# Seventy-two weight columns instead of 128 in one product of a gated feed-forward kernel

## The chip, the cores and the metric

The kernel runs on one NeuronCore of a Trainium2 chip; the other seven are idle. The metric is the device time of one execution in microseconds (us). TensorE multiplies a stationary operand (the weights, which a LDWEIGHTS instruction puts into the array) with a moving operand (the data, which a MATMUL streams through it) and adds the result up in a PSUM bank. The profile calls the matmuls PE and the weight loads PEld; DVE is VectorE, ACT is ScalarE, POOL is GpSimd, SP issues the DMAs.

## The reference

A softmax over seven taps weights seven neighbouring positions of `x` (an attention with a window of 7, eight heads), and the result goes through a gated feed-forward layer with 1,536 hidden channels and 192 output channels, for 16,384 positions. Cut to what matters here, with `a` the output of the window:

```python
w = softmax(weight_gen, axis=-1)                    # 7 taps, 8 heads
a[t] = sum_k w[t, :, k] * x_pad[t + k]              # 16384 x 192
gate = 1.0 / (1.0 + np.exp(-(a @ w_gate)))          # 192 -> 1536
val  = a @ w_val
out  = (gate * val) @ w_out                         # 1536 -> 192
```

## The kernel before, in words

**Tiling.** Positions are cut into 32 blocks of 512, hidden channels into 12 groups of 128. One block with one group is a unit, 384 in all. Per unit, `main_jobs` multiplies the 192 channels of `a` with the gate's and the value's weights (two PSUM banks, `g` and `v`); ACT makes the sigmoid `sg`, DVE the product `h`; and `out_jobs` multiplies `h` with the output weights into two further banks, `ph` for output channels 0 to 127 and `pt` for channels 128 to 191, which add up over the 12 units of a block.

**Two parts of each number.** The operands of the matmuls are of type fp32r, and each number is split into a high and a low part of that type. `hh` and `hl` are those of `h`; a weight tile `W[f]` holds high columns and, from column `LO` on, low ones. For the first 128 output channels there are three products, named head: high weights with `hh`, low weights with `hh`, high weights with `hl`. For the last 64 channels high and low weights stand side by side and make one 128-column operand, `both_`: columns 0 to 63 are high, 64 to 127 low. Two products are then enough, named tail: `both_` with `hh`, and `both_` with `hl`. The upper half of `pt` (low weights) is added to the lower at the end (`evac`).

**Row halves.** Each matmul contracts only 64 rows. The array holds two at a time, one on rows 0 to 63 (`LOW`) and one on rows 64 to 127 (`UP`). The program always issues them alternately, so that they run in pairs; such a pair is called a slot. A unit has 18 main and 10 output matmuls, hence 14 slots. `period(s)` writes them: the main products of unit `s`, mixed with the output products of unit `s - 2`, first those of the upper half (`up`, beside gate products) and later those of the lower half (`low`, beside value products). Each half of the array thus gets one tail product with `hl` per unit.

**Turns.** Both halves write `ph` and `pt`. Where the writing half changes, `emit` puts a tiny memset on POOL (`seen`, line 839) that waits for the last matmul of one half, and the first of the other waits for it.

**Order.** A planner (`Plan.run`) fixes the order of all engines' instructions when the program is built, from estimated durations; `SLOT` is the estimate for a slot. `emit` (line 841 issues every one of these matmuls) writes the jobs of a step in the order of the lists that `out_jobs` and `main_jobs` return. `ending` writes the last two units' output products without main products beside them.

Of the kernel before, what the change touches and what calls it, by code (L numbers as in the profile page):

```python
# [217 lines left out]
def conv_gated_ffn(ctx: ExitStack, tc: tile.TileContext, xt, wg, wcat, outT):  # L218
# [12 lines left out]
    nc = tc.nc  # L231
# [7 lines left out]
    R = P // 2  # L239
# [546 lines left out]
    def keys(u):  # L786
        n, f = units[u]
        return dict(
            A=("A", n), As=("As", n), T=("T", n), g=("gv", u, 0), v=("gv", u, 1), sg=("sg", u),
            h=("h", u), hh=("hh", u), hl=("hl", u), ph=("ph", n), pt=("pt", n),  # L790
        )
# [12 lines left out]
    def out_jobs(u, r, head_first, last=False):  # L804
        k, (n, f) = keys(u), units[u]
        rows = (LOW, UP)[r]
        w = W[f][rows, :]
        hi, lo = w[:, CB : CB + P], w[:, LO + CB : LO + CB + P]
        both_ = w[:, CB + P : CB + 2 * P]
        head = [(k["ph"], hi, "hh"), (k["ph"], lo, "hh"), (k["ph"], hi, "hl")]  # L810
        tail = [(k["pt"], both_, "hh"), (k["pt"], both_, "hl")]
        begin = f == 0 and r == 1
        jobs = []
        for part in (head, tail) if head_first else (tail, head):
            for i, (dst, w, t) in enumerate(part):
                jobs.append(
                    (dst, w, k[t], rows, None, begin and i == 0,
                     last and i == len(part) - 1)
                )
        return jobs  # L820
# [7 lines left out]
    def emit(slots):  # L828
        def f(buf, e):
            for pair in slots:  # L830
                for job in pair:
                    if job is None:
                        continue
                    dst, w, t, rows, x, start, stop = job
                    m = buf[t][rows, :] if x is None else buf[t][rows, x, :]
                    r, prior = writer.get(dst, (rows.start, None))
                    turn = None
                    if r != rows.start:
                        turn = nc.gpsimd.memset(seen, 0.0)  # L839
                        tc.add_manual_dep(turn.ins, prior.ins.name, SYNC, reason="end of a turn")  # L840
                    ins = nc.tensor.matmul(buf[dst], w, m, start=start, stop=stop)  # L841
                    if turn is not None:
                        tc.add_manual_dep(ins.ins, turn.ins.name, SYNC, reason="next turn")
                    writer[dst] = (rows.start, ins)

        return f
# [10 lines left out]
    def period(s):  # L857
# [8 lines left out]
        if u < 0:  # L866
            jobs, gv = list(zip(G, V)), [k["g"], k["v"]]
            for i in range(3):
                b = c = pe(
                    jobs[3 * i : 3 * i + 3], conv_op[f]["done"] + ready[n, i],  # L870
                    alloc=[] if i else [("gv", g) for g in gv],
                    uses=[xs[i]] + (gv if i else []), due=due[s, 2],
                )
        else:
            last = fo == NF - 1
            up = out_jobs(u, 1, True)
            low = out_jobs(u, 0, True, last)
            hs = [ko["hh"], ko["hl"]]
            po = [ko["ph"], ko["pt"]]
            gv = [k["g"], k["v"]]  # L880
            pe(
                list(zip(G[:2], V[:2])), deps, alloc=[("gv", k["g"]), ("gv", k["v"])], uses=xs,
                due=due[s, 0],
            )
            pe(
                list(zip(G[2:7], up)), conv_op[fo]["done"] + u_op[u],
                alloc=[("ph", po[0]), ("pt", po[1])] if fo == 0 else [],
                uses=xs + hs + gv + ([] if fo == 0 else po), due=due[s, 1],
            )
            b = pe(list(zip(G[7:], V[2:4])), [], uses=xs + gv, due=due[s, 2])  # L890
            c = pe(list(zip(low, V[4:])), [], uses=xs + hs + po + gv, due=due[s, 3])
            if last:
                evac(no, [c])
# [24 lines left out]
    def ending():  # L918

        a, b = len(units) - 2, len(units) - 1  # L920
        la, ua = out_jobs(a, 0, True), out_jobs(a, 1, False)
        lb, ub = out_jobs(b, 0, True), out_jobs(b, 1, False, True)
        lb[4] = lb[4][:-1] + (True,)
        ub[1] = ub[1][:-1] + (False,)
        X = None
        ka, kb = keys(a), keys(b)
        po = [ka["ph"], ka["pt"]]
        cf = conv_op[units[b][1]]["done"] + conv_op[units[a][1]]["done"]
        pe(
            list(zip(la, [ua[0], ua[1], X, ua[2], ua[3]])), cf + u_op[a],  # L930
            uses=[ka["hh"], ka["hl"]] + po, due=due[len(units), 3],
        )
        c = pe(
            list(zip(lb + [X, X], [ub[0], ub[1], X, ua[4], ub[2], ub[3], ub[4]])), u_op[b],
            uses=[ka["hh"], ka["hl"], kb["hh"], kb["hl"]] + po, due=due[len(units) + 1, 3],
        )
        evac(units[b][0], [c])
# [108 lines left out]
```

## Time and profile before

| | |
|---|---|
| median of 3 runs | 1303.37 us (1303.14 to 1305.34) |
| the profiled execution: span | 1304.0 us |
| PE busy | 1269.9 us (97%), 10,860 matmuls |
| PEld busy | 1068.8 us (82%), 10,860 weight loads |
| DVE, ACT, POOL busy | 1040.3, 615.6, 131.2 us |
| chain that ended last | PE 78%, DVE 17%, rest 5% |
| mean granted clock of TensorE | 0.992 |

The busy times are sums over the whole span, and matmuls overlap one another, so that 97% does not tell by itself what limits PE. Timelines are read in order of start: the distance from one slot's start to the next is the pace. A clock of 1.00 is the upper of TensorE's two levels (2.4 GHz), 0.50 the lower (1.2 GHz).

### The profile page before, as it was taken

Reading aid. Unit: us, or ns where it says so; the run is one execution under the profiler, and the core shown is the slowest. Engines: PE = TensorE matmul, PEld = TensorE weight load, DVE = VectorE, ACT = ScalarE, POOL = GpSimd, SP = SyncE. Lnnn points to the kernel's source line nnn. Section 1 sums busy time; section 2 is a strip of 40 time slices with the busy share of each in tenths; the row PEclk is TensorE's granted clock in tenths of the full one; section 3 lists DMA queues with packets and bytes.
Section 4 is the critical chain, followed back from the end, with each engine's and each line's share of the span. In section 5 each row is a group of like instructions: output and inputs, shape, how many; then the busy total and the mean of one; then the engine's idle time right before and its main releaser. Section 6 shows DMA issues by size and latency. Waiting matters only on the chain.

```text
span 1304.0 us, 29730 instructions
## 1 busy us (share of the span) xinstructions
PE 1269.9 (97%) x10860; PEld 1068.8 (82%) x10860; DVE 1040.3 (80%) x1904; ACT 615.6 (47%) x1040; POOL 131.2 (10%) x1477
## 2 busy tenths in 40 slices
PE   4989999999999999999999999999999999999998
PEld 2768788888877888888888888888888888888886
DVE  8889979999998788777778877777887777786443
ACT  4855745455454444444444444444444444444443
POOL 0000011111100111111111111111111111111110
PEclk9999999999989999999999999999999999999999
DMA  4675189798864454344445434444543444211100
GB/s 123 168 192 117 40 170 170 167 188 164 193 146 116 115 134 120 89 118 114 115 117 134 115 96 114 117 114 119 134 116 91 118 116 111 57 38 38 37 13 14
DMA packets 56482, 148.94 MB, mean 114 GB/s; under 512 B 10640, under 2 KB 28176, under 8 KB 56336
## 3 DMA queue, kind: packets, MB, share of 16 engines
q1 hardware_dynamic: 56336, 147.04, 48.1%
q8 instruction: 86, 1.41, 0.5%
q14 instruction: 60, 0.49, 0.1%
HBM read 108.86 MB, written 16.14 MB: 96 GB/s over the span
## 4 chain that ended last, share of the span: by engine, by line
PE 78%; DVE 17%; issue 2%; ACT 2%; DMA 1%; POOL 0%; DVEq 0%; SPq 0%; POOLq 0%; ACTq 0%
PE bank L841 76%; DVE acc L638 3%; DVE h L899 3%; DVE hl L905 3%; DVE prod L624 3%; DMA x<-in_x 1%; PE bank L408 1%; DVE m L458 1%; DVE acc L624 0%; DVE prod L677 0%; DVE acc L697 0%; DVE m L484 0%; DVE w L465 0%; DVE osb L951 0%; DVE cr L394 0%
## 5 line engine op out<-in xcount | busy, mean ns | idle before, releaser
L841 PE MATMUL bank<-hh,W 64*128 64x512 f32 x2304 | 772.2, 389 | 2.9 <-ACT hh L902 2.1
L841 PE MATMUL bank<-As,W 64*128 64x512 f32 x2304 | 650.2, 389 | 1.3 <-ACT As L732 0.7
L841 PE MATMUL bank<-T,W 64*128 64x512 f32 x2304 | 647.9, 388 | 2.0 <-ACT T L775 1.8
L841 PE MATMUL bank<-hl,W 64*128 64x512 f32 x1536 | 596.1, 389 | 1.8 <-DVE hl L905 1.6
L902 ACT CAST hh<-h 128x512 fp32r<-128x512 f32 x384 | 238.4, 621 | 518.0 <-DVE h L899 516.6
L841 PE MATMUL bank<-A,W 64*128 64x512 f32 x2304 | 474.8, 389 | 2.8 <-DVE h L899 2.4
L841 PEld LDWEIGHTS bank<-hh,W 64*128 64x128 f32 x2304 | 425.0, 185 | 43.2 <-issue 3.6
L841 PEld LDWEIGHTS bank<-T,W 64*128 64x128 f32 x2304 | 425.4, 185 | 41.1 <-ACT T L775 2.5
L841 PEld LDWEIGHTS bank<-As,W 64*128 64x128 f32 x2304 | 424.2, 185 | 40.2 <-ACT As L735 1.3
L899 DVE TENSOR_TENSOR h<-bank,sg 128x512 f32<-128x512 f32 x384 | 263.8, 687 | 158.2 <-PE bank L841 151.9
L905 DVE TENSOR_TENSOR hl<-h,hh 128x512 fp32r<-128x512 f32 x384 | 264.1, 688 | 86.8 <-ACT hh L902 83.0
L841 PEld LDWEIGHTS bank<-A,W 64*128 64x128 f32 x2304 | 291.2, 185 | 43.4 <-DVE h L899 3.3
L841 PEld LDWEIGHTS bank<-hl,W 64*128 64x128 f32 x1536 | 283.9, 185 | 29.8 <-DVE hl L905 4.6
L896 ACT ACTIVATE sg<-bank 128x512 f32<-128x512 f32 x384 | 229.8, 599 | 111.7 <-PE bank L841 107.3
L839 POOL MEMSET seen<- 1x1 f32 x1471 | 130.5, 89 | 1166.0 <-PE bank L841 1165.8
L638 DVE TENSOR_TENSOR acc<-acc,prod 128x512 f32<-128x512 f32 (+1 forms) x372 | 204.1, 552 | 0.9
L624 DVE TENSOR_TENSOR prod<-x,wb 128x512 f32<-128x512 f32 x186 | 122.8, 685 | 0.0
L624 DVE TENSOR_TENSOR prod<-xt,wt 128x256 f32<-128x256 f32 x186 | 77.4, 418 | 0.0
L759 DVE TENSOR_TENSOR T<-acc,T 64x256 fp32r<-64x256 f32 x64 | 26.7, 417 | 1.4 <-ACT T L756 0.4
L408 PE MATMUL bank<-ce,eye 128*128 128x512 f32 (+1 forms) x48 | 19.7, 496 | 7.3 <-DVE prod L677 6.0
L948 ACT COPY ev<-bank 64x512 f32<-64x512 f32 x32 | 18.7, 584 | 16.9 <-PE bank L841 16.9
L756 ACT CAST T<-acc 64x256 fp32r<-64x256 f32 x64 | 25.8, 403 | 0.8
(54 smaller groups left out, 359.9 us busy)
## 6 DMA issues: line engine op xcount, KB each, us to landing
wb<-ws SPq DMA_DIRECT2D x62, 896.0 KB
wt<-ws SPq DMA_DIRECT2D x62, 448.0 KB
As<-A SPq DMA_DIRECT2D x56, 256.0 KB
x<-in_x SPq DMA_DIRECT2D x32, 259.0 KB
out<-osb SPq DMA_DIRECT2D x32, 256.0 KB
T<-T SPq DMA_DIRECT2D x56, 128.0 KB
raw<-in_w SPq DMA_DIRECT2D x12, 576.0 KB
xt<-in_x SPq DMA_DIRECT2D x64, 65.5 KB
```

The source lines that it names most:

```text
L408: nc.tensor.matmul(dst, eye[:, 0].bitcast(F32), buf[E].bitcast(F32)[:, a:z], start=True, stop=False)
L624: nc.vector.tensor_tensor(out=buf[prod(k)][:, :cols].rearrange("p (i t) -> p i t", t=M2), in0=buf[X][:, k : k + cols].rearrange("p (i t) - ...
L638: ENG[e].tensor_tensor(out=a, in0=a, in1=buf[prod(k)][:, :cols], op=ALU.add)
L756: nc.scalar.copy(buf[T][rows, 0, own], buf[ACT_][rows, :M2])
L759: ENG[e].tensor_tensor(out=buf[T][rows, 1, own], in0=buf[ACT_][rows, :M2], in1=buf[T][rows, 0, own].bitcast(F32), op=ALU.subtract,)
L839: turn = nc.gpsimd.memset(seen, 0.0)
L841: ins = nc.tensor.matmul(buf[dst], w, m, start=start, stop=stop)
L896: nc.scalar.activation(out=buf[k["sg"]], in_=buf[k["g"]], func=AF.Sigmoid)
L899: nc.vector.tensor_tensor(out=buf[k["h"]], in0=buf[k["v"]], in1=buf[k["sg"]], op=ALU.mult)
L902: nc.scalar.copy(buf[k["hh"]], buf[k["h"]])
L905: ENG[e].tensor_tensor(out=buf[k["hl"]], in0=buf[k["h"]], in1=buf[k["hh"]].bitcast(F32), op=ALU.subtract)
L948: nc.scalar.copy(buf[EV][LOW, :], buf[PT][UP, :])
```

## The change

The tail product with `hl` takes only the first 72 of the 128 columns of `both_`: the 64 high ones and 8 of the low ones. Its result goes to partitions 0 to 71 of `pt`. The low weights' product with the low part of `h` is thereby left out for 56 of 64 channels. For the lower half (`r == 0`) the two tail products change places, so that the full-width one stands last.

```diff
@@ out_jobs
-        tail = [(k["pt"], both_, "hh"), (k["pt"], both_, "hl")]
+        tail = [(k["pt"], both_, "hh"), (k["pt"], both_[:, : R + 8], "hl")]
+        if r == 0:
+            tail.reverse()
@@ emit
-                    ins = nc.tensor.matmul(buf[dst], w, m, start=start, stop=stop)
+                    ins = nc.tensor.matmul(
+                        buf[dst][: w.shape[-1]], w, m, start=start, stop=stop
+                    )
```

`R` is 64. Every other engine's instructions, and all waits, are the same in the same order; 1,152 of PE's rows differ, three per unit. On PE, in the second half of one unit's slots in the middle of the program, the rows before are these (a number after a name is that of a buffer, `W_6` belongs to main products and `W_4` to output products; each row gives the output's shape and the semaphores waited for):

```order
L841 MATMUL bank_113<-As1_87,W_6_120 128x512
L841 MATMUL bank_113<-hl1_98,W_4_118 128x512
L841 MATMUL bank_113<-T1_89,W_6_120 128x512
L841 MATMUL bank_113<-hh1_95,W_4_118 128x512 [waits Pool_49]
L841 MATMUL bank_113<-T1_89,W_6_120 128x512
L841 MATMUL bank_113<-hl1_98,W_4_118 128x512
L841 MATMUL bank_113<-T1_89,W_6_120 128x512
L841 MATMUL bank_113<-A1_85,W_7_121 128x512 [waits Activation_49]
```

And now, on PE at the same place:

```order
L843 MATMUL bank_113<-As1_87,W_6_120 128x512
L843 MATMUL bank_113<-hl1_98,W_4_118 128x512
L843 MATMUL bank_113<-T1_89,W_6_120 128x512
L843 MATMUL bank_113<-hl1_98,W_4_118 72x512 [waits Pool_49]
L843 MATMUL bank_113<-T1_89,W_6_120 128x512
L843 MATMUL bank_113<-hh1_95,W_4_118 128x512
L843 MATMUL bank_113<-T1_89,W_6_120 128x512
L843 MATMUL bank_113<-A1_85,W_7_121 128x512 [waits Activation_49]
```

The narrow product stands where the wide one with `hh` stood, with the same wait for POOL, and the one with `hh` comes a slot later; in the upper half's slots only the width of one row changes.

## Rows read from the trace of the kernel before

**Rows 1.** The page's first part: busy us, share of the span, instructions.

```profile
PE 1269.9 (97%) x10860; PEld 1068.8 (82%) x10860; DVE 1040.3 (80%) x1904; ACT 615.6 (47%) x1040; POOL 131.2 (10%) x1477
```

**Rows 2.** The chain that ended last, from 411 us on: start, length, what.

```profile
411.15 883.20 PE bank L841 x7776
1294.35 0.04 issue
```

**Rows 3.** Stretches of time: length, busy us (instructions) by engine, clock, DMA share, GB/s.

```profile
412.00:414.00 2.00, 2.00 (x12) 1.62 (x10) 0.77 (x2) 0.60 (x1) 0.09 (x1) 0.50 0.00 0
417.00:800.00 383.00, 383.00 (x3382) 327.83 (x3380) 298.25 (x542) 171.79 (x293) 40.79 (x463) 1.00 0.47 115
800.00:1294.00 494.00, 494.00 (x4362) 422.75 (x4360) 354.69 (x634) 219.19 (x372) 52.50 (x596) 1.00 0.34 84
```

**Rows 4.** Groups from 417 to 1294 us: busy, mean ns, idle before.

```profile
L841 PE MATMUL bank<-hl,W 64*128 64x512 f32 x1106 | 426.9, 386 | 0.0
...
L841 PEld LDWEIGHTS bank<-hl,W 64*128 64x128 f32 x1106 | 203.5, 184 | 18.0
```

**Rows 5.** Timeline of PE, upper clock: start us, length us, instruction.

```profile
801.18 0.39 PE L841 MATMUL bank<-As,W 64*128 64x512 f32 x1
801.19 0.39 PE L841 MATMUL bank<-hh,W 64*128 64x512 f32 x1
801.41 0.39 PE L841 MATMUL bank<-As,W 64*128 64x512 f32 x1
801.42 0.39 PE L841 MATMUL bank<-hl,W 64*128 64x512 f32 x1
801.64 0.39 PE L841 MATMUL bank<-T,W 64*128 64x512 f32 x1
801.65 0.39 PE L841 MATMUL bank<-hh,W 64*128 64x512 f32 x1
```

**Rows 6.** Timeline of PEld, the same place.

```profile
801.41 0.18 PEld L841 LDWEIGHTS bank<-T,W 64*128 64x128 f32 x1
801.42 0.18 PEld L841 LDWEIGHTS bank<-hh,W 64*128 64x128 f32 x1
```

**Rows 7.** Timeline of PE at the lower clock level.

```profile
412.39 0.62 PE L841 MATMUL bank<-A,W 64*128 64x512 f32 x1
...
413.67 0.62 PE L841 MATMUL bank<-As,W 64*128 64x512 f32 x1
```

**Rows 8.** Timeline of PEld: loads for 64-wide, then for line 841's matmuls.

```profile
40.32 0.19 PEld L409 LDWEIGHTS bank<-W,eye 128*128 128x128 f32 x1
40.43 0.19 PEld L410 LDWEIGHTS bank<-cr,eye 128*128 128x128 f32 x1
40.67 0.18 PEld L841 LDWEIGHTS bank<-A,W 64*128 64x128 f32 x1
40.67 0.18 PEld L841 LDWEIGHTS bank<-hh,W 64*128 64x128 f32 x1
40.77 0.19 PEld L841 LDWEIGHTS bank<-As,W 64*128 64x128 f32 x1
```

**Rows 9.** Timeline of PE, the same place and the slots behind it.

```profile
40.46 0.28 PE L410 MATMUL bank<-cr,eye 128*128 128x64 f32 x1
40.67 0.50 PE L841 MATMUL bank<-A,W 64*128 64x512 f32 x1
40.67 0.50 PE L841 MATMUL bank<-hh,W 64*128 64x512 f32 x1
41.01 0.40 PE L841 MATMUL bank<-As,W 64*128 64x512 f32 x1
41.01 0.40 PE L841 MATMUL bank<-hh,W 64*128 64x512 f32 x1
41.25 0.39 PE L841 MATMUL bank<-As,W 64*128 64x512 f32 x1
```

**Rows 10.** Timeline of PE in the ending: matmuls without a partner.

```profile
1298.15 0.62 PE L841 MATMUL bank<-hh,W 64*128 64x512 f32 x2
1298.62 0.39 PE L841 MATMUL bank<-hl,W 64*128 64x512 f32 x1
```

**Rows 11.** Timeline of POOL: the memset of a turn and its wait.

```profile
801.01 0.09 POOL L839 MEMSET seen<- 1x1 f32 x1 [0.37 <-PE bank L841]
```

## The prediction

> **What bounds the kernel now.** The first part of the page [rows 1] has PE busy for 97% of the span and DVE for 80%; this says only where to look. The chain of waits decides: from 411.15 us it is one piece of 883.20 us and 7,776 matmuls, all of line 841, and behind it only the ending is left [rows 2]. In the table of stretches PE is busy without a break from 417 to 1294 us at a granted clock of 1.00, while DVE is busy for 78% and 72% of it [rows 3], and the groups of that stretch show no idle time before any matmul [rows 4]. So for 68% of the span (883.20 of 1304.0) the time is a count of slots times the pace of a slot, and nothing else on the chip matters. Before 411 us PE and DVE take turns on the chain; the same slots run there, and I count what a slot gains or loses there as an upper bound only.
>
> The pace: 883.20 / 3,888 slots is 0.2272 us. The timeline shows it slot by slot: the two matmuls of a slot start 0.01 us apart, and the next pair starts 0.23 us later, whatever the operand is (801.18, 801.41, 801.64) [rows 5]. At the lower clock level three slots take 413.67 - 412.39 = 1.28 us, 0.427 each [rows 7], at a clock of 0.50 [rows 3]. Were all of it paced by TensorE's clock, the upper level would halve it to 0.2133. The measured pace is 0.0139 us longer. A slot is thus 0.213 us of streaming 512 columns and some 0.014 us of something that the lower clock hides, call it the change-over.
>
> Is it the weight load? A load takes 0.184 us by the record [rows 4], starts as the matmul ahead of it starts, and has ended some 0.04 us before the slot after it begins (801.41 + 0.18 against 801.64) [rows 5, 6]. Even that length is mostly latency: where the matmuls are only 64 wide, a load follows the one before after 0.11 us (40.32, 40.43) [rows 8], so that this is what a 128-column load costs where nothing covers it. The loads of the two halves run at the same time: after a stop two start at 40.67, the next at 40.77 [rows 8], and both halves' second matmuls start together at 41.01 [rows 9]. One half's matmuls without a partner keep no better pace: two from 1298.15 and the next at 1298.62 are two steps of 0.235 [rows 10]. A load therefore has about 0.12 us to spare in each slot, and the partner costs nothing.
>
> **The change part by part.**
>
> *Narrower loads.* 768 loads, one per unit in each half, have 72 columns in place of 128. If the cost goes with columns, 0.11 us becomes 0.062, and 768 x 0.048 = 37 us of load work goes. All of it lies under the matmul ahead, with 0.12 us to spare, so I put it at 0. The cover is missing only in the ending, where a load after a stop lies open: at most five times 0.05 us, 0.25 us by this estimate, and I take 0.1.
>
> The Trainium skill ("TensorE: Matmul & The Clock Gate", section on LDWEIGHTS) gives the load's time as its columns at 1.2 GHz: 107 ns for 128, 60 for 72. The step of 0.11 us in rows 8 agrees with the first; no row here has the second. By the page the saving would be 47 ns a load, hidden all the same.
>
> *Narrower matmuls.* The same 512 columns of data stream through, so 0.213 us of the slot stays. Whether the change-over depends on the width of the weights the trace can't tell, since every load in it has 128 columns. From above: it does not, gain 0. From below: it vanishes for the narrow ones, 384 x 0.0139 = 5.3 us (each half has one per unit, and both halves must gain, or the faster waits for its partner; where only the slots from 411 us count, 278 units, 3.9 us). In between, in proportion to columns: 56/128 x 0.0139 = 6.1 ns, times 384, 2.3 us. I take 0: the change-over disappears at the lower clock [rows 7], so it isn't steps of the array, one per weight column, and the records fit a fixed time beside the stream better.
>
> *The swap in the lower half.* The first tail product of the half waits for the POOL memset of a turn. The memset for it starts at 801.01 and takes 0.09 us [rows 11]; the load that stands there starts at 801.42 [rows 6], 0.32 us later. The narrow product now takes this place with the same wait, and its operand `hl` was already used by the slot before. The turn to the other half ends with the same slot as before. Cost 0. Nothing is moved on DVE, ACT, POOL or SP.
>
> *Sum.* Span of the profiled execution 1304.0 - 0.1 = 1303.9; that execution lies 0.6 us above the median of 1303.37, so the median stays at 1303.3.
>
> **The rivals.**
>
> *The change-over follows the width.* 1303.4 - 2.3 = 1301.1 in proportion, 1298.1 if it goes away wholly. For it: nothing in the trace has another width. Against it: rows 7.
>
> *The loads set the pace.* Then each half gains 0.048 us per unit: 384 x 0.048 = 18.4 us, 1285.0. For it: PEld is busy for 85.6% of 417 to 1294 us (327.83 + 422.75 of 877) [rows 3]. Against it: the load is over before the slot begins [rows 5, 6], and one half alone, with half as many loads, is no faster [rows 10]. The Trainium skill ("Perfetto Trace Analysis", section "Identifying the Most-Contended Engine") advises to judge TensorE by the busy share of LDWEIGHTS rather than by that of the matmuls; by that rule this rival would lead, but 0.184 us of record for 0.11 us of work makes the share too high here.
>
> *A narrow matmul breaks the rhythm: slower.* After a stop the first slots run at 0.24 and 0.23 us (41.01 to 41.25) [rows 9], although nothing is waited for, and settle at 0.227 later. If a load of another width upsets the same thing, each narrow one costs 0.24 - 0.227 = 0.013 us; the halves have theirs in different slots, so both count: 768 x 0.013 = 10 us, 1313.4. If no slot settled any more, at some 0.232 us in the mean, it would be 5,376 x 0.005 = 27 us, 1330. It decides as soon as one slot in seven is disturbed by over 0.003 us. Against it: the pace in the stretch doesn't move although operands, banks and halves change from slot to slot.
>
> *A narrow matmul counts as another shape of the array: slower.* From the 128-row matmuls to the 64-row pairs the load comes 0.24 us after the last in place of 0.11, and then lies open for 0.11 more (first pair 0.34 long in place of 0.23) [rows 8, 9]: 0.24 us per switch. In and out twice a unit that is 4 x 0.24 x 384 = 369 us, 1672. Against it: the built program gives the narrow ones the same tile of 64 x 128 as all others. The Trainium skill ("TensorEngine Tiling (Array Packing)", "Key Properties") has that a change of tiling mode drains the engine while another tile of the same mode doesn't; with up to 64 columns there would be a mode of that width, and 72 are over it. Rows 8 agree that a change of mode costs.
>
> *The change doesn't take hold:* the loads stay 128 wide on the chip. The time is then the forecast's, too.
>
> **How the numbers follow.** About 0.2%, 2.6 us, is what a measurement of this kernel can tell from no change. Chances: nothing moves (with the case that it doesn't take hold) 0.76; the change-over shrinks in proportion 0.09, vanishes 0.03; loads set the pace 0.03; rhythm 0.06; another shape 0.03. The proportional case of 2.3 us lies within 0.2% for most of its chance (0.07). This gives faster 0.08, same 0.83, slower 0.09. The likeliest case gives 1303.3. The range takes in the spread of the runs of before (1303.1 to 1305.3) above, and the proportional case below: 1300.9 to 1305.5. It leaves out 0.06 below and 0.09 above.
>
> **What would show it.** In the profile after: matmuls of `hl` in two groups, 768 of them 72 wide; their loads with records shorter by up to 0.05 us and nothing else moved; slots still 0.227 us apart, the chain's last long piece still some 883 us; POOL's memsets 0.3 us ahead of the load that waits. I am wrong about the loads if slots with a narrow product are shorter by 0.05 us, wrong about the change-over if they are shorter by some 0.006 to 0.014, and the rhythm rival is right if the slot behind a narrow product is 0.23 to 0.24 us long or the two matmuls of a slot no longer start at a constant distance. A gap of 0.2 us about each narrow product would show the drain.

## The result and the profile after

The changed kernel takes 1312.85 us (median of 5 runs, 1311.66 to 1312.94), the one before 1303.37 (1302.38 to 1305.34): a ratio of 1.006 with a 95% interval of 1.0046 to 1.0074. It is slower by 0.6%, where no change was forecast. The profiled execution has a span of 1310.2 us (before 1304.0).

The first part of the page after, as in [rows 1] (busy us, share, instructions):

```profile
PE 1276.3 (97%) x10860; PEld 1129.0 (86%) x10860; DVE 1043.1 (80%) x1904; ACT 616.3 (47%) x1040; POOL 131.9 (10%) x1477
```

The chain that ended last, as in [rows 2] (start, length, what):

```profile
411.55 888.98 PE bank L843 x7776
1300.53 0.04 issue
```

It is the same long piece of 7,776 matmuls. It is 5.8 us longer, although the one before had a stretch at the lower clock in it [rows 3, 7] and this one has none. So the time went where PE alone sets the pace, and not into a wait: the stretches, as in [rows 3], still show PE busy without a break at a clock of 1.00, only with fewer matmuls in the same time (3,354 and 4,326 in place of 3,382 and 4,362).

```profile
417.00:800.00 383.00, 383.00 (x3354) 342.02 (x3352) 297.92 (x540) 169.43 (x289) 40.57 (x459) 1.00 0.47 115
800.00:1294.00 494.00, 494.00 (x4326) 441.10 (x4324) 353.94 (x631) 218.22 (x371) 52.25 (x591) 1.00 0.34 84
```

28 matmuls are a unit. From the starts of the matmuls between 430 and 1250 us, the same product of consecutive units is 3,173.3 ns apart before and 3,200.0 after: 26.7 ns a unit. The groups from 417 to 1294 us, as in [rows 4], show that the change did take hold, and that the load became shorter by 46 ns (the two groups of `hl` and their loads, mean ns behind the busy time):

```profile
L843 PE MATMUL bank<-hl,W 64*72 64x512 f32 x548 | 213.7, 390 | 0.0
...
L843 PE MATMUL bank<-hl,W 64*128 64x512 f32 x548 | 212.1, 387 | 0.0
...
L843 PEld LDWEIGHTS bank<-hl,W 64*128 64x128 f32 x548 | 100.8, 184 | 3.5
L843 PEld LDWEIGHTS bank<-hl,W 64*72 64x72 f32 x548 | 75.3, 138 | 3.5
```

Where the 26.7 ns are, PE's timeline tells, to be held against [rows 5] (start, length, instruction; the first of each pair is the upper half's here, the second the lower's; the last row is the lower half's own narrow product):

```profile
802.29 0.39 PE L843 MATMUL bank<-hh,W 64*128 64x512 f32 x1
802.32 0.39 PE L843 MATMUL bank<-T,W 64*128 64x512 f32 x1
802.52 0.39 PE L843 MATMUL bank<-hl,W 64*72 64x512 f32 x1
802.55 0.39 PE L843 MATMUL bank<-T,W 64*128 64x512 f32 x1
802.75 0.39 PE L843 MATMUL bank<-A,W 64*128 64x512 f32 x1
802.77 0.39 PE L843 MATMUL bank<-T,W 64*128 64x512 f32 x1
802.99 0.39 PE L843 MATMUL bank<-As,W 64*128 64x512 f32 x1
803.00 0.39 PE L843 MATMUL bank<-hh,W 64*128 64x512 f32 x1
...
803.68 0.39 PE L843 MATMUL bank<-T,W 64*128 64x512 f32 x1
803.68 0.39 PE L843 MATMUL bank<-hl,W 64*72 64x512 f32 x1
```

The upper half's matmuls start at 802.52, 802.75 and 802.99: 0.23 and 0.24 us. In nanoseconds, from one narrow product of that half to the next, its 14 steps are 231, 236, 228, 233, 231, eight of 226 or 227, and 228. The lower half does nearly the same around its own narrow product, five slots later (803.68). Meanwhile the other half keeps its 227: the two matmuls of a pair drift from 30 ns apart to 5 and back, where before they stayed 10 ns apart. A narrow product is therefore followed by some five slow slots, as the stop in [rows 9] is by slow ones, and then the half settles again.

### The profile page after: what moved, and what is told of

Read it like the earlier page. It is cut to its first block, busy times and chain, and to the rows that moved or that the text cites. A ratio compares the mean times of both kernels' runs of the same rounds, so it can differ in the third digit from the quotient of the medians.

```text
span 1310.2 us, 29730 instructions
## 1 busy us (share of the span) xinstructions
PE 1276.3 (97%) x10860; PEld 1129.0 (86%) x10860; DVE 1043.1 (80%) x1904; ACT 616.3 (47%) x1040; POOL 131.9 (10%) x1477
## 4 chain that ended last, share of the span: by engine, by line
PE 86%; DVE 9%; DMA 3%; issue 1%; ACT 1%; SPq 0%; POOL 0%; DVEq 0%; POOLq 0%; ACTq 0%
PE bank L843 84%; DMA wb<-ws 2%; DVE h L903 1%; DVE hl L909 1%; DVE prod L624 1%; DVE acc L638 1%; PE bank L408 1%; DMA w<-in_weight_gen 1%; DVE m L458 1%; DVE prod L677 0%; DVE w L465 0%; DVE m L484 0%; SPq L601 0%; PE bank L410 0%; DVE T L759 0%
## 5 line engine op out<-in xcount | busy, mean ns | idle before, releaser
L843 PE MATMUL bank<-hl,W 64*128 64x512 f32 (+1 forms) x1536 | 537.7, 390 | 2.2 <-DVE hl L909 1.7
L843 PE MATMUL bank<-A,W 64*128 64x512 f32 x2304 | 483.1, 391 | 2.6 <-DVE h L903 2.4
L843 PEld LDWEIGHTS bank<-A,W 64*128 64x128 f32 x2304 | 299.4, 185 | 30.1 <-DVE h L903 3.3
L843 PEld LDWEIGHTS bank<-hl,W 64*128 64x128 f32 (+1 forms) x1536 | 247.6, 161 | 14.4 <-DVE hl L909 3.9
L759 DVE TENSOR_TENSOR T<-acc,T 64x256 fp32r<-64x256 f32 x64 | 26.7, 417 | 1.4 <-ACT T L756 0.4
```

Of the source, the lines that this page charges most:

```text
L759: ENG[e].tensor_tensor(out=buf[T][rows, 1, own], in0=buf[ACT_][rows, :M2], in1=buf[T][rows, 0, own].bitcast(F32), op=ALU.subtract,)
L843: ins = nc.tensor.matmul(buf[dst][: w.shape[-1]], w, m, start=start, stop=stop)
```

## Experiments

The measure for all of them is the length of a unit where PE alone sets the pace, taken as above, and beside it the number of matmuls between 420 and 1280 us. All unit lengths turned out to be whole steps of 6.67 ns away from 3,173.3, within 0.6 ns (e5 and e6 are means over units of unlike length). All kernels have the clock at 1.00 in that window. Each ratio is against runs of the kernel before on the same chip, and so tells more than a difference of medians.

| kernel | unit, ns | steps | matmuls | ratio of times (95%) |
|---|---|---|---|---|
| before | 3173.3 | 0 | 7592 | |
| changed | 3200.0 | 4 | 7528 | 1.006 (1.0046 to 1.0074) |
| e1: swap alone, 128 wide | 3173.3 | 0 | 7592 | 1.0008 (0.9995 to 1.0020) |
| e2: 72 wide, no swap | 3200.0 | 4 | 7528 | 1.0058 (1.0043 to 1.0073) |
| e5: 72 in the lower half only | 3199.4 | 4 | 7531 | 1.0064 (1.0048 to 1.0080) |
| e6: two of 72 in a row, lower half | 3187.1 | 2 | 7558 | 1.0037 (1.0026 to 1.0048) |
| e12: 64 wide | 3193.3 | 3 | 7545 | 1310.1 us, one run (before, on that chip: 1302.9 to 1304.6) |
| e8: 80 wide | 3193.3 | 3 | 7544 | 1.0062 (1.0047 to 1.0077) |
| e3: 96 wide | 3226.7 | 8 | 7468 | 1.0140 (1.0123 to 1.0156) |
| e9: 112 wide | 3193.3 | 3 | 7544 | 1.0055 (1.0033 to 1.0076) |
| e4: 120 wide | 3180.0 | 1 | 7576 | 1.0022 (1.0013 to 1.0032) |
| e7: everything 72 wide | 3226.7 | 8 | 7466 | 1.0158 (1.0143 to 1.0173) |
| e11: a main product 72 wide | 3200.0 | 4 | 7528 | 1.0064 (1.0048 to 1.0080) |
| e10: 128 wide, 480 positions | 3206.7 | 5 | 7513 | 1.0087 (1.0069 to 1.0105) |

**Is it the width or the swap?** e1 keeps the swap alone, e2 the width alone (the swap stays only in the last of a block's 12 units).

```diff
 e1, in out_jobs of the changed kernel
-        tail = [(k["pt"], both_, "hh"), (k["pt"], both_[:, : R + 8], "hl")]
+        tail = [(k["pt"], both_, "hh"), (k["pt"], both_, "hl")]
 e2
-        if r == 0:
+        if r == 0 and f == NF - 1:
```

> All weights 128 columns wide again, only the order swap of the lower half's two tail products is kept. Theory 'width' (each narrow product costs its half 27 ns, as the trace of the changed kernel shows: 3.200 us per unit instead of 3.173): the pace returns to 3.173 us per unit and the time to that of before, 1303 us. Rival 'swap' (the other order, with two products of hl in a row, breaks the rhythm): 3.200 us per unit, 1313 us.

> 72 columns in both halves, but the lower half keeps the order hh, hl except in the last unit of each block. Theory 'width': 3.200 us per unit, 1313 us. Rival 'swap': 3.173 us per unit, about 1304 us.

The stretch from 420 to 1280 us of e1 and of e2 (length, busy us and instructions by engine; PE's is the first):

```profile
420.00:1280.00 860.00, 860.00 (x7592) 711.42 (x7590) 644.35 (x1162) 383.44 (x651) 91.81 (x1038) 1.00 0.41 99
```

```profile
420.00:1280.00 860.00, 860.00 (x7528) 845.80 (x7526) 642.79 (x1157) 379.50 (x647) 90.88 (x1029) 1.00 0.41 99
```

e1 passes as many matmuls as the kernel before, e2 as few as the changed one. The swap costs nothing; the width is the cause.

**Do the halves add up?** e5 leaves the upper half 128 wide.

```diff
-        tail = [(k["pt"], both_, "hh"), (k["pt"], both_[:, : R + 8], "hl")]
+        tail = [(k["pt"], both_, "hh"), (k["pt"], both_[:, : R + 8] if r == 0 else both_, "hl")]
```

> The narrow product in the lower half only, the upper half's is 128 wide. Theory 'each half for itself' (a half loses 27 ns per narrow product and the halves run beside each other, so the slower one sets the unit): still 3.200 us per unit, 1313 us. Rival 'one after the other' (each narrow product delays both halves by 13 ns): 3.187 us per unit, 1308 us.

It came out at 3,199.4 ns and 1.0064: one narrow product in one half costs as much as one in each. The halves lose beside each other, 26.7 ns per narrow product. The program issues both halves' matmuls in turn, and the upper half, though it has no narrow product, shows slow slots of its own (228, 231, 236, 228, 233 and 230 ns in one unit) and loses the same 26.7 ns. That the order of issue drags it along is likely, but no run here shows it.

**Is it the step from one width to another?** e6 makes the head's product with `hl` narrow as well, next to the tail's, in the lower half and in 11 of 12 units. e7 makes all of them narrow; a memset of the banks, 3.5 us on DVE, stands ahead of its first matmuls.

```diff
 e6, on top of e5
             tail.reverse()
+            if f < NF - 1:
+                head[2] = (k["ph"], hi[:, : R + 8], "hl")
 e7, on top of e1
+                    w = w[:, :72]
                     ins = nc.tensor.matmul(
```

> In the lower half only, the head's product with hl is narrow too (channels 72 to 127 of that product are left out) in 11 of 12 units, so that two narrow products follow each other in that half; the upper half is 128 wide. Theory 'transition' (what costs is the step from one width to another, 13 ns each way): no more than with one narrow product in the lower half, 3.200 us per unit, 1313 us. Rival 'narrow' (each narrow product costs 27 ns, whatever stands beside it): 3.227 us per unit, 1322 us.

> Every matmul of the units is 72 columns wide, main products too (so channels 72 to 127 of every product are left out), in the order of the changed kernel; a memset of the banks is added at the start, some 4 us beside DMA waits. No width changes between neighbours. Theory 'transition' (only a change of width costs): slots 226.67 ns apart as before, about 1305 us. Theory 'a narrow load costs two steps each time': slots of 253 ns, about 1440 us. Rival of the prediction 'the change-over follows the width': slots of 220.6 ns, about 1273 us.

Neither theory held. Two narrow products in a row cost half as much as one (13.8 ns, against 26.7 to 53 expected). And with no change of width anywhere, e7 never settles: the stretch of 420 to 1280 us and PE's timeline in it are

```profile
420.00:1280.00 860.00, 860.00 (x7466) 526.06 (x7464) 642.19 (x1155) 377.27 (x643) 90.17 (x1022) 1.00 0.40 99
```

```profile
1001.05 0.39 PE L845 MATMUL bank<-hh,W 64*72 64x512 f32 x1
...
1001.28 0.39 PE L845 MATMUL bank<-hh,W 64*72 64x512 f32 x1
...
1001.51 0.38 PE L845 MATMUL bank<-hl,W 64*72 64x512 f32 x1
...
1001.74 0.39 PE L845 MATMUL bank<-hh,W 64*72 64x512 f32 x1
```

The steps of a half go round in seven, 234, 235, 231, 229, 226, 229 and 229 ns, 230.5 in the mean against 226.7. PEld is busy for 526 us in place of 736, and the kernel is 1.6% slower: the loads are not what limits it (in this the prediction was right), and the change-over does not shrink with the width. Smaller differences in PEld's busy time say little, since time in which both halves load counts once: e1, with the loads and the pace of the kernel before, has 711 us, and e2, with some shorter loads, 846.

**Which widths?** The same edit as the change with 96, 80, 120, 112 and 64 columns.

> As the changed kernel, with 96 columns instead of 72 in the narrow products of both halves. Slots that run undisturbed are 226.67 ns apart, 17 steps of 13.33 ns, and a unit of the changed kernel is longer by two such steps. Theory 'step of 32' (a width that is a multiple of 32 columns keeps the rhythm): 3.173 us per unit, 1303 us. Theory 'any narrower width' (a narrow load as such costs two steps): 3.200 us per unit, 1313 us.

> 80 columns instead of 72: a multiple of 16, not of 32. If a load of 128 columns is 8 steps of 13.33 ns (the 0.11 us of a bare load), 80 columns are 5 whole steps and 72 are four and a half. Theory 'step of 16': 3.173 us per unit, 1303 us, and the same for 96. Theory 'step of 32': as 72, 3.200 us per unit, 1313 us, while 96 costs nothing. Theory 'any narrower width': 3.200 us per unit, 1313 us.

> 120 columns instead of 72: seven and a half steps. Theories 'step of 16' and 'step of 32': disturbed as with 72, 3.187 to 3.200 us per unit, 1308 to 1313 us. Theory 'amount' (the cost goes with the columns left out, 8 here against 56): 3.177 us per unit, 1304.5 us. Theory 'any narrower width': 3.200 us per unit, 1313 us.

> 112 columns instead of 72 in both halves. So far a unit gained 27 ns at 72 columns, 20 at 80, 53 at 96 and 7 at 120, so the amount does not follow the columns left out. Theory 'each width has its own way back into the rhythm': some multiple of 6.7 ns between 7 and 53, 1305 to 1323 us, not foreseen more closely. Rival 'multiples of 16 columns above 96 keep the rhythm': 3.173 us per unit, 1303 us.

> 64 columns instead of 72: the program gives these the shape of a 64 x 64 tile, all others 64 x 128. Theory 'change of shape drains': two changes to it and two back per unit at 0.24 us each, 369 us more, about 1670 us. Rival 'only another width': 7 to 53 ns per unit, 1305 to 1323 us.

Steps of 32 or 16 columns don't explain it: 96 is the worst (8 steps), 80 and 112 cost 3. The columns left out don't either: from 120 down to 64 the steps are 1, 3, 8, 3, 4, 3. With 120 columns one slot is longer, the one ahead of the narrow product, and the next is settled again (PE's timeline of e4, the second of each pair; from `hh` to the narrow `hl` it is 233 ns, then 227):

```profile
1001.28 0.39 PE L843 MATMUL bank<-hl,W 64*128 64x512 f32 x1
...
1001.51 0.39 PE L843 MATMUL bank<-hh,W 64*128 64x512 f32 x1
...
1001.75 0.39 PE L843 MATMUL bank<-hl,W 64*120 64x512 f32 x1
...
1001.97 0.39 PE L843 MATMUL bank<-A,W 64*128 64x512 f32 x1
```

With 64 columns the built program does change the tile's shape, to 64 x 64, and no pause follows. PEld's and PE's timelines of e12 around the narrow product of the lower half:

```profile
1000.57 0.13 PEld L843 LDWEIGHTS bank<-hl,W 64*64 64x64 f32 x1
1000.58 0.18 PEld L843 LDWEIGHTS bank<-T,W 64*128 64x128 f32 x1
1000.79 0.18 PEld L843 LDWEIGHTS bank<-hh,W 64*128 64x128 f32 x1
```

```profile
1000.57 0.39 PE L843 MATMUL bank<-hl,W 64*128 64x512 f32 x1
...
1000.79 0.40 PE L843 MATMUL bank<-hl,W 64*64 64x512 f32 x1
...
1001.03 0.39 PE L843 MATMUL bank<-hh,W 64*128 64x512 f32 x1
```

The steps are 0.22 and 0.24 us and the loads lie under the matmuls ahead, as ever. It costs a little less than 72 columns, and as much as 80 and 112.

**Is it the place, or the loads alone?** e11 makes a main product narrow and leaves the output products wide. e10 has 128 columns everywhere and streams fewer positions in the tail product with `hl`.

```diff
 e11, in main_jobs, on top of e1
-                jobs.append((k["gv"[r]], W[f][rows, col : col + P], k[t], rows, x))
+                wide = R + 8 if len(jobs) == 4 else P
+                jobs.append((k["gv"[r]], W[f][rows, col : col + wide], k[t], rows, x))
 e10, in emit, on top of e1
+                    cols = 480 if dst[0] == "pt" and t[0] == "hl" else N
-                        buf[dst][: w.shape[-1]], w, m, start=start, stop=stop
+                        buf[dst][:, :cols], w, m[:, :cols], start=start, stop=stop
```

> The output products are 128 wide; instead one main product per half and unit, the fifth of nine, is 72 wide (channels 72 to 127 of that product are left out). Theory 'width' without regard to place: 27 ns per unit as with the tail's, 3.200 us, 1313 us. Rival 'place' (the output products are special, by their bank, their turns or the weights' address): another amount or none, 3.173 us per unit, 1303 us.

> Weights 128 wide everywhere; instead, the tail product with hl streams 480 of the 512 positions in both halves (the last 32 positions' product is left out), 13.3 ns less streaming, one step. Theory 'the width of the load' (only loads of another width upset the rhythm): each half is 13 ns shorter per unit, 3.160 us, about 1298 us. Rival 'any odd one out' (a matmul that differs from its neighbours in any size upsets it): no shorter than before, 3.173 to 3.200 us per unit, 1303 to 1313 us.

e11 gives 3,200.0 ns, to the nanosecond what the tail's narrow product gives: between these two places, bank, turns and the weights' address make no difference. e10 is the strongest of the results. Each half has 13.3 ns less to stream in every unit, and a unit gets 33.3 ns longer:

```profile
420.00:1280.00 860.00, 860.00 (x7513) 775.69 (x7511) 643.43 (x1158) 380.18 (x649) 91.17 (x1027) 1.00 0.41 99
```

```profile
1003.54 0.37 PE L844 MATMUL bank<-hl,W 64*128 64x480 f32 x1
...
1003.75 0.39 PE L844 MATMUL bank<-hh,W 64*128 64x512 f32 x1
...
1003.99 0.39 PE L844 MATMUL bank<-A,W 64*128 64x512 f32 x1
...
1004.22 0.66 PE L844 MATMUL bank<-A,W 64*128 64x512 f32 x4
```

The short one is 0.21 us long, as it should be, and then come 0.24, 0.23 and so on. So it isn't the load of the weights as such: a matmul that differs from its neighbours in either size upsets the pace of its half, in most of these runs for several slots.

**Is there an order in these slots?** Of the kernel before, PE's timeline goes on behind the stop of [rows 9] like this (one half only):

```profile
41.25 0.39 PE L841 MATMUL bank<-As,W 64*128 64x512 f32 x1
...
41.48 0.39 PE L841 MATMUL bank<-As,W 64*128 64x512 f32 x1
...
41.72 0.39 PE L841 MATMUL bank<-T,W 64*128 64x512 f32 x1
...
41.95 0.38 PE L841 MATMUL bank<-T,W 64*128 64x512 f32 x1
...
42.18 0.39 PE L841 MATMUL bank<-T,W 64*128 64x512 f32 x1
...
42.41 0.39 PE L841 MATMUL bank<-hh,W 64*128 64x512 f32 x1
```

In nanoseconds, from the slot that starts at 41.01 us on, the steps are 240, 235, 233, 236, 224, 231, 236, 228, 233, 230, and then 227. The disturbed halves run through the end of this same series (means over 60 us of each trace). Behind 480 positions it is 235, 233, 236, 224, 231, 236, 228, 233, 231; behind 96 columns the same, after two slots of 230; behind 72 columns (e11 too) 231, 236, 228, 232, 231; behind 80, 112 and 64 columns 236, 228, 233, 231. Over 226.67 ns each, what is left of the series adds up to 47 ns in the first two cases, 25 in the third and 21 in the last. With 13.3 ns less to stream for 480 positions, and a few nanoseconds in the slots ahead of the product elsewhere, these are the losses of the table: an odd matmul puts its half back to some place in the settling series, and the place decides the loss. What sets the place, no run tells. 120 columns and the two of 72 in a row (229, 234, 231) do not follow the series.

## Why the prediction was wrong, point by point

**What bounds the kernel: right.** The time is a count of slots times the pace of a slot. 278 units lie in the long piece, 278 x 26.7 ns = 7.4 us; all 384 would be 10.2 us. The ratio's interval, 1.0046 to 1.0074, is 6.0 to 9.6 us of 1303.4, so most units count, those before 411 us in part. The long piece grew by 5.8 us and not by 7.4, since only the one before has eight slots at 0.427 us [rows 7] in place of 0.227, some 1.6 us. The same holds along the table: 8 steps of 6.67 ns make 20.5 us over all units, and e3 and e7 measured ratios of 1.014 and 1.016, 18 and 21 us (e7 with its memset in it).

**Narrower loads hidden: right.** The load became shorter by 46 ns, and nothing was gained; in e7 all loads did, and the time rose. The Trainium skill ("TensorE: Matmul & The Clock Gate", section on LDWEIGHTS) has the load go with its columns at 1.2 GHz, 47 ns for 56 columns; the records of 184 and 138 ns agree in their difference of 46, while each is some 78 ns over what that rule gives for its width (107 and 60). The Trainium skill's advice to judge TensorE by the busy share of LDWEIGHTS ("Perfetto Trace Analysis", "Identifying the Most-Contended Engine") is about the distance from the best possible time, and names MFU (the achieved share of the peak arithmetic rate) beside it. As a sign that the loads set the pace, which the prediction made of it for a rival, the share does not serve here: in e7 it falls from 86% to 61% and the kernel is slower. One support of the prediction was weak: the two steps of 0.235 us in [rows 10] stand 0.5 us behind a wait of PE for POOL, so they are slots behind a stop and do not tell the pace of one half alone.

**The swap at no cost: right** (e1). So were the wait for POOL (its memset ends at 803.12 us, and the load that waits for it starts at 803.46) and the other engines: nothing but PE's pace moved.

**"Narrower matmuls", the change-over: this is the step that failed.** I put its ends at no effect ("it does not, gain 0") and at a gain of 5.3 us, and none at a loss, because I took the 13.9 ns over 213.3 as a price that each slot pays by itself. It is not. 226.67 ns is the pace to which a sequence of equal matmuls settles, and a slot's length depends on the sizes of the matmuls around it: where the term had 0, a narrow product cost its half 26.7 ns (e5, e11). The 13.9 ns were a little off as well: the 883.20 us have the slots at the lower clock in them, and 226.67 is 13.3 over 213.3. Leaving out a loss there had no reason behind it: no row showed a matmul of another size in the middle of settled ones, and [rows 9] showed slots of 0.23 to 0.24 us that nothing explained.

**The rivals.** "A narrow matmul breaks the rhythm" is what happened, at 0.06. Its price of 10 us was nearly right, for two errors that cancel: I gave each narrow product 13 ns and added the halves up, while it is 27 ns and the halves lose side by side (e5). What I held against it, that the pace stays the same though operands, banks and halves change, was true and beside the point: none of these is a size. The loads as the pace (1285) and the change-over by width (1301.1) are refuted by e7. "Another shape" (1672) was wrong in its price as well: e12 does change the tile's shape and pays 20 ns a unit, not 0.96 us. The Trainium skill ("TensorEngine Tiling (Array Packing)", "Key Properties") has a change of tiling mode drain the engine; between 64 x 128 and 64 x 64, e12 shows no such pause, and the measurement decides. The pause of [rows 8] stands where the number of rows changes, from 128 to 64, and that may be another matter; it wasn't tried.

**The signs named ahead** were the right ones: the slots behind a narrow product are 0.23 to 0.24 us long, and the two matmuls of a pair no longer start at a constant distance.

**What stays open** is what keeps the pace. The runs show that the settled pace of equal matmuls with 128 columns and 512 positions is 226.67 ns, that with 72 columns throughout there is no settled pace but a round of seven, that unit lengths move in whole steps of 6.67 ns, and that the loss per odd matmul goes 1, 3, 8, 3, 4, 3 steps from 120 down to 64 columns, and by 2 for two of 72 in a row. Why the steps are of that size, and why the slots come back through that one series, no run here tells. Nor do the runs part the number of weight columns from the number of PSUM partitions written, which always go together. No version of the change was faster than the kernel before, and none of these results points to one.

## What to carry to other kernels

In a kernel that is one long train of equal matmuls, count a matmul of another size, in weight columns or in streamed positions, as a possible loss of some tens of nanoseconds until a run has shown otherwise, even if it has less to do; in no run here was less work in some matmuls a gain while their number stayed. A constant that is worked out from a trace in which nothing varies is a constant of that trace: give its dependence on a size that never varied a bound on both sides. Where a trace shows slow steps that nothing explains (here behind a stop), take the state that they stand for as a rival with a real chance.

## What the runs showed of the hardware that was not expected

- Slots settle at 226.67 ns at the upper clock, and at 0.427 us at the lower one [rows 7]; half of that is 213.3, and the upper clock's slots are 13.3 ns over it.
- Behind a stop the slots are 224 to 240 ns long for about ten slots before they are 226.67 again, and behind most of the odd-sized matmuls they go through the end of the same series; 120 columns lengthen one slot only, the one ahead. Unit lengths differ in whole steps of 6.67 ns.
- Streaming 480 in place of 512 positions once per unit and half made a unit 33.3 ns longer.
- A tile of 64 x 64 between tiles of 64 x 128 cost 20 ns a unit, less than 72 columns in the common shape, and showed no pause.
